# The inverse turn through DRAM to partitions 4 apart, a last stage on 64×32 tiles, and half of the loop's matrices made on the chip

## The chip, the cores and the metric

The kernel runs on one core of one Trainium2 chip. The metric is the device time of one execution in microseconds (us). All data are float32. TensorE (PE in the profile) multiplies matrices, its weight loads are listed apart (PEld). VectorE is DVE, ScalarE is ACT, GpSimd is POOL. SyncE (SP) does no arithmetic here, it issues transfers. POOL issues transfers too, on a queue of its own.

## The reference

Two branches read the same 2048×512 input and are mixed by a gate for each row:

```python
x = A_u
g = _sigmoid((x * gate_w).sum(-1, keepdims=True))
a = _A_ref(x, ...)   # K from 128 complex modes per channel; y = causal convolution of u with K; + u * Dskip
b = _B_ref(x, ...)   # gelu(x @ w1 + b1) @ w2 + b2, 512 -> 1792 -> 512
return g * a + (1 - g) * b
```

In `_A_ref`, `K = einsum(Cc, exp(dt*A*l), dt*Bc).real` gives 2048 taps for each of the 512 channels, and the convolution is done in the reference with a Fourier transform of length 4096.

## The kernel before

The kernel has two parts. `front` computes the taps, the dense branch, the gates, and the first stage of the forward transform of signal and taps. Its instructions are ordered by a planner (`Plan`), which the change leaves alone. `conv` does the rest, in an order written out by hand. Everything below is about `conv`.

The transform is split into 32 frequencies of the first stage (`n` in the code, taken in the order of `k0_order`) and 64 points of the second. `front` leaves the first stage's results in DRAM (`t2_d`), one block of 128 rows for each `n`. `conv` then works in three steps.

**The loop** (`for s in range(16)`) takes two `n` at a time. `fetch(n)` brings the block (`t2`, 512 KB) and, for every fourth `n`, the constant matrices of four `n` (`cc`, 512 KB) through SP. A block has 12 buffers. `signal(s)` and `taps(s)` (both through `pair`) multiply 128×64 matrices into two halves of a PSUM bank. ScalarE copies the taps' result to SBUF (`k`). `product(s)` is six VectorE instructions, the complex product of signal and taps. `inverse(s)` multiplies it back with 64-row matrices into `pa`. `turn(s)` copies each `pa` to `sa` on ScalarE (four buffers) and sends it off. In one iteration TensorE does `signal(s+1)`, `taps(s+2)`, `inverse(s)`. The product of `s` runs on VectorE meanwhile.

**The turn.** The last stage must sum over `n`, so all 32 `sa` tiles have to become one tile `t3` whose partitions run over `n`. Each `sa` has 128 rows, made of 4 parts `j` (real or imaginary, times two row halves `i`) of 32 rows `q`. In `t3`, one partition holds one `(n, j)` with all 32 `q` one behind another, 64 KB. `settle` does this in `GROUPS`: the first 28 `sa` are stored to `t4_d` in DRAM through SP, and when a group of 8, 8, 8 or 4 is complete, POOL reads it into `t3` at partitions 4, 4, 4 or 8 apart. The last four `sa` go straight from SBUF into 4 partitions each, 32 apart, also on POOL's queue, which works in order.

**The last stage** is 32 matrix products of 128 rows by 64 columns (half of each matrix is zero, since the two halves `i` don't mix), two for each of 16 output tiles. VectorE adds each, times the gate, to the dense result (`mo`), which `dense(k)` has read back from `out`, and SP stores it. Two of the dense branch's sums (42 products of 128×128 by 512) are left by `front` as a list `late`. `rest(n)` works off `n` entries (three products each): 4 in iteration 14, 4 in iteration 15, and the other 6 behind the loop.

PSUM tiles of the tag `pu` have four buffers, `pa` and `pk` two each.

Of the kernel before, what the change touches and what calls it, by code (L numbers as in the profile page):

```python
# [17 lines left out]
P = 128  # L18
L = 2048
# [68 lines left out]
def k0_order():  # L88
    return [8 * (n % 4) + n // 4 for n in range(32)]


# [12 lines left out]
def constants():  # L104


    def om(e4):
        a = 2.0 * np.pi * (np.asarray(e4) % (4 * L)) / (4 * L)
        return np.cos(a), -np.sin(a)

    k0 = np.arange(32)
    p = np.arange(32)
    q = np.asarray(slot_q())
    k1 = np.arange(64)
    qn = np.arange(64)
# [10 lines left out]
    g1 = np.zeros((2, 2, 32, 2, 32))  # L126
    for i in range(2):
        g1[i, 0, :, i] = er.T / L
        g1[i, 1, :, i] = ei.T / L
    g1 = g1.reshape(4, 32, 64)  # L130
    rows = np.zeros((P, 64))
    for first, count, at, step in GROUPS:
        for i in range(count):
            for j in range(4):
                rows[at + step * (4 * i + j)] = g1[j, k0_order()[first + i]]
    g1 = rows


    f2 = np.zeros((32, 2, 64, 2, 64))
    g2 = np.zeros((32, 2, 64, 64, 2))  # L140
    for k in range(32):
        er, ei = om(4 * (q[:, None] * k + 32 * np.outer(q, k1)) + q[:, None])
        f2[k, 0, :, 0], f2[k, 1, :, 0], f2[k, 0, :, 1], f2[k, 1, :, 1] = er, -ei, ei, er
        er, ei = om(4 * (qn[None] * k + 32 * np.outer(k1, qn)) + qn[None])
        g2[k, 0, :, :, 0], g2[k, 1, :, :, 0] = er, ei
        g2[k, 0, :, :, 1], g2[k, 1, :, :, 1] = -ei, er
    g2 = g2.reshape(32, P, 32, 2, 2).transpose(0, 1, 3, 4, 2)

    ko = k0_order()
    f2 = f2.reshape(32, P, P)[ko]  # L150
    g2 = g2[ko].reshape(16, 2, 2, 64, P).transpose(0, 2, 1, 3, 4).reshape(32, P, P)
    c2 = np.stack([f2, g2], 1).reshape(8, 4, 2, P, P).transpose(0, 3, 1, 2, 4)
# [111 lines left out]
def gated_mix(  # L264
# [22 lines left out]

    dt_d = dr.tile([1, D], F32, name="dt_d")
    t2_d = dr.tile([32, P, 2, D], F32, name="t2_d")
    t4_d = dr.tile([32, P, D], F32, name="t4_d")  # L290

# [738 lines left out]
    def conv(pool, ps, late):  # L1030

        t3 = pool.tile([P, 32, D], F32, name="t3", bufs=1)
        g1t = pool.tile([P, 64], F32, name="g1t", bufs=1)
        ko = k0_order()
        c4s, t2s = {}, {}

        def fetch(n):
            if n % 4 == 0:
                c4s[n // 4] = pool.tile([P, 4, 2, P], F32, tag="cc", name=f"cc{n}", bufs=3)
                nc.sync.dma_start(c4s[n // 4], c2[n // 4])  # L1040
            t2s[n] = pool.tile([P, 2, D], F32, tag="t2", name=f"t2{n}", bufs=N_T2)
            nc.sync.dma_start(t2s[n], t2_d[ko[n]])
            if n == 7:
                nc.sync.dma_start(g1t, g1)


# [3 lines left out]
        def pair(s, r, c, out):  # L1050

            for i in range(2):
                n = 2 * s + i
                w = c4s[n // 4][:, n % 4, 0, 64 * c : 64 * c + 64]
                nc.tensor.matmul(out[64 * i : 64 * i + 64], w, t2s[n][:, r], start=True, stop=True)  # L1055
# [17 lines left out]
        def product(s):  # L1073

            (ur, ui), (kr, ki) = pus.pop(s), fac.pop(s)
            z = [pool.tile([P, D], F32, tag=f"z{i}", name=f"z{s}{i}", bufs=1) for i in range(4)]
            v = [pool.tile([P, D], F32, tag=f"v{i}", name=f"v{s}{i}", bufs=2) for i in range(2)]
# [8 lines left out]
        def inverse(s):  # L1086
# [4 lines left out]
            for c in range(2):  # L1091
                n = 2 * s + c
                w = c4s[n // 4][:, n % 4, 1]
                for i in range(2):
                    r = slice(64 * i, 64 * i + 64)
                    nc.tensor.matmul(pas[2 * s + i], w[r], v[c][r], start=(c == 0), stop=(c == 1))  # L1096

        def settle(n, sa):

            for first, count, at, step in GROUPS:  # L1100
                if count > 1 and first <= n < first + count:
                    nc.sync.dma_start(t4_d[n], sa)
                    if n == first + count - 1:
                        rows = t4_d[first : n + 1].rearrange("n (j q) d -> (n j) q d", j=4)
                        nc.gpsimd.dma_start(t3[at:P:step], rows)
                elif n == first:
                    nc.gpsimd.dma_start(t3[at:P:step], sa)
# [28 lines left out]
        for n in range(N_T2):  # L1136
            fetch(n)
        nxt = N_T2
        taps(0)
        signal(0)  # L1140
        taps(1)
        for s in range(16):

            for n in range(nxt, min(2 * s + N_T2, 40)):
                (fetch if n < 32 else dense)(n if n < 32 else n - 32)
                nxt = n + 1
            product(s)
            if s + 1 < 16:
                signal(s + 1)
            if s + 2 < 16:  # L1150
                taps(s + 2)
# [9 lines left out]
        for t in range(16):  # L1161
            pb = ps.tile([P, D], F32, tag="pu", name=f"pb{t}", bufs=4)
            for b in range(2):
                nc.tensor.matmul(pb[64 * b : 64 * b + 64], g1t, t3[:, 2 * t + b], start=True, stop=True)  # L1164
            z, g = mos[t // 2][:, t % 2], gate[:, 0, t : t + 1]
            nc.vector.scalar_tensor_tensor(z, pb, g, z, ALU.mult, ALU.add)
            if t >= 12:
                nc.sync.dma_start(out[t], z)
            elif t % 2 == 1:
                nc.sync.dma_start(out[t - 1 : t + 1].rearrange("s p d -> p s d"), mos[t // 2])  # L1170

# [19 lines left out]
def layout(inputs):  # L1191
# [6 lines left out]

    xs = xpq.reshape(32, 16, 4, D).transpose(1, 2, 0, 3).reshape(16, P, D)
    xt = xs.reshape(NSB, SB, 4, P).transpose(0, 3, 2, 1)  # L1200
# [46 lines left out]
```

## Time and profile before

| what | us |
|---|---|
| median of 3 runs (lowest to highest) | 574.27 (571.66 to 575.11) |
| the profiled execution, its own time | 573.21 |
| its span, first to last instruction | 571.4 |
| `front`, up to the first product of `conv` | 434.8 |
| from there to the first `inverse` | 12.7 |
| from the first `inverse` to the end of the last | 86.7 |
| from there to the first product of the last stage | 15.9 |
| the last stage, to VectorE's last instruction | 17.7 |
| the last store and the end | 3.5 |

The stages' ends are read from the chain of waits and from the timeline of TensorE. The prediction shows the lines. In the table of stages a column is an engine's busy time in a stretch with the number of its instructions, then the clock that TensorE was granted (1.00 is full), the mean busy share of the 16 DMA engines, and GB/s. One matrix product of float32 shows as two MATMUL records. A source line such as L1164 is a line of the kernel before.

### The profile page before, as it was taken

The numbers are of one execution on the slowest core, as the hardware profiler recorded it, in microseconds if no ns is written. First come the engines' busy times: TensorE is split into PE (matmuls) and PEld (weight loads), VectorE is DVE, ScalarE is ACT, GpSimd is POOL, SyncE is SP. The second block draws the span as 40 slices with busy tenths as digits, with TensorE's granted clock in tenths as the row PEclk, the third lists the DMA queues.
The fourth block names the chain that finished last, engine by engine and source line by source line (L and its number), as shares of the span: only waits on it lengthen the run. The fifth ranks groups of instructions, "written<-read, shape, count | busy, mean of one in ns | idle before, by whom it ended". The sixth has DMA issues, their size and how long they took to land.

```text
span 571.4 us, 11957 instructions
## 1 busy us (share of the span) xinstructions
PE 541.3 (95%) x4746; PEld 403.8 (71%) x4746; DVE 449.4 (79%) x844; ACT 361.8 (63%) x606; POOL 32.2 (6%) x69
## 2 busy tenths in 40 slices
PE   7859999999999999999999999999998999999646
PEld 7738878888887888888888889898884333324412
DVE  5899998998989989998998898988512766675116
ACT  4998656899676799987669857477443334333100
POOL 2000000000000000000120201101010000000200
PEclk9969999999999999999999999999998999999959
DMA  8868735232864232649531358223269899999846
GB/s 267 306 216 304 240 111 186 75 130 86 255 209 167 95 130 93 201 141 252 137 82 33 95 122 156 75 38 80 35 143 334 320 322 396 380 420 452 230 97 258
DMA packets 77396, 109.50 MB, mean 192 GB/s; under 512 B 39014, under 2 KB 42218, under 8 KB 77228
## 3 DMA queue, kind: packets, MB, share of 16 engines
q1 hardware_dynamic: 71484, 87.89, 45.2%
q0 software_dynamic: 5856, 20.85, 14.6%
q8 instruction: 37, 0.61, 0.4%
q14 instruction: 19, 0.16, 0.1%
HBM read 63.09 MB, written 44.57 MB: 188 GB/s over the span
## 4 chain that ended last, share of the span: by engine, by line
PE 77%; DMA 14%; DVE 2%; ACT 2%; SPq 1%; issue 1%; POOL 0%; POOLq 0%; ACTq 0%
PE pk L647 11%; PE acc L905 9%; PE ph L857 9%; PE ph L859 8%; PE ph L858 8%; PE acc L907 8%; PE acc L906 8%; DMA t_d<-sa 5%; PE pu L388 4%; PE p2k L1055 3%; PE pb L1164 3%; DMA t<-t_d 3%; PE pa L1096 3%; PE p2u L1055 3%; DMA t<-sa 2%; DMA ld<-in_xt_dram 2%
## 5 line engine op out<-in xcount | busy, mean ns | idle before, releaser
L857 PE MATMUL ph<-xh,wh 128*128 128x256 f32 x448 | 128.0, 286 | 1.5 <-DVE wh L736 1.5
L859 PE MATMUL ph<-xh,wl 128*128 128x256 f32 x448 | 127.0, 283 | 0.6 <-DVE wl L740 0.5
L858 PE MATMUL ph<-xlo,wh 128*128 128x256 f32 x448 | 126.5, 282 | 0.0
L857 PEld LDWEIGHTS ph<-xh,wh 128*128 128x128 f32 x448 | 85.1, 190 | 7.5 <-issue 4.0
L905 PE MATMUL acc<-wh,hh 128*128 128x512 f32 x210 | 87.8, 418 | 0.4 <-ACT hh L877 0.4
L858 PEld LDWEIGHTS ph<-xlo,wh 128*128 128x128 f32 x448 | 85.1, 190 | 1.7
L859 PEld LDWEIGHTS ph<-xh,wl 128*128 128x128 f32 x448 | 85.1, 190 | 1.2 <-DVE wl L740 1.2
L906 PE MATMUL acc<-wl,hh 128*128 128x512 f32 x210 | 83.2, 396 | 0.0
L907 PE MATMUL acc<-wh,hl 128*128 128x512 f32 x210 | 82.9, 395 | 0.0
L874 ACT ACTIVATE ph<-ph,b1t 128x256 f32<-128x256 f32 x112 | 50.6, 452 | 28.7 <-PE ph L859 26.9
L647 PE MATMUL pk<-y,xc 128*32 128x64 f32 x2048 | 61.5, 290 | 0.0
L647 PEld LDWEIGHTS pk<-y,xc 128*32 128x32 f32 x2048 | 57.2, 136 | 4.0 <-issue 2.5
L905 PEld LDWEIGHTS acc<-wh,hh 128*128 128x128 f32 x210 | 39.8, 190 | 19.8 <-issue 11.9
L887 DVE TENSOR_TENSOR hl<-ph,hh 128x512 fp32r<-128x512 f32 (+1 forms) x62 | 38.2, 618 | 13.1 <-ACT hh L877 12.5
L907 PEld LDWEIGHTS acc<-wh,hl 128*128 128x128 f32 x210 | 39.8, 190 | 9.7 <-DVE hl L887 0.8
L611 DVE TENSOR_TENSOR y<-y,ea 128x64 f32<-128x64 f32 (+4 forms) x80 | 45.3, 566 | 0.4
L906 PEld LDWEIGHTS acc<-wl,hh 128*128 128x128 f32 x210 | 39.9, 190 | 5.8
L666 ACT COPY sk<-pu 128x512 f32<-128x512 f32 x32 | 33.9, 1129 | 15.5 <-PE pu L388 15.3
L1112 ACT COPY sa<-pa 128x512 f32<-128x512 f32 x32 | 17.7, 588 | 36.8 <-PE pa L1096 21.1
L877 ACT CAST hh<-ph 128x512 fp32r<-128x512 f32 (+1 forms) x62 | 33.0, 532 | 10.9 <-PE acc L906 9.1
L456 DVE TENSOR_TENSOR xt<-xc,zz 128x256 f32<-128x256 f32 (+2 forms) x48 | 37.2, 775 | 1.9 <-ACT xc L582 1.6
L1055 PE MATMUL p2k<-t,cc 128*64 128x512 f32 x128 | 35.4, 613 | 3.0 <-DMA t<-t_d 1.7
(138 smaller groups left out, 891.5 us busy)
## 6 DMA issues: line engine op xcount, KB each, us to landing
t<-t_d SPq DMA_DIRECT2D x32, 512.0 KB, 7.9
t_d<-st SPq DMA_DIRECT2D x32, 256.0 KB, 3.3
t_d<-sk SPq DMA_DIRECT2D x32, 256.0 KB, 4.2
t_d<-sa SPq DMA_DIRECT2D x28, 256.0 KB, 6.9
ld<-in_xt_dram SPq DMA_DIRECT2D x16, 256.0 KB, 3.9
xh_d<-xh SPq DMA_DIRECT2D x8, 512.0 KB, 3.8
xl_d<-xlo SPq DMA_DIRECT2D x8, 512.0 KB, 5.5
ux<-in_xl_dram SPq DMA_DIRECT2D x16, 256.0 KB, 3.4
```

The source lines that it names most:

```text
L456: vec(2 * m, lambda: vv.tensor_mul(t, a, br), due, [ka, *kb], [kt])
L611: nc.vector.tensor_mul(both(n, 64 - 3 * n, n), both(0, 64 - n, n), an)
L647: nc.tensor.matmul(pks[q][32 * j : 32 * j + 32, gg], x[:, r, :, ch], y[:, r, :, ch], start=(r == 0), stop=(r == 1), skip_group_check=True,)
L857: nc.tensor.matmul(p, h, xh[xk][:, d], start=(d == 0), stop=False)
L858: nc.tensor.matmul(p, h, xlo[xk][:, d], start=False, stop=False)
L859: nc.tensor.matmul(p, lo, xh[xk][:, d], start=False, stop=(d == 3))
L874: nc.scalar.activation(phs[q][:, n], phs[q][:, n], AF.Gelu_apprx_tanh, bias=b1t[:, f : f + 1])
L887: nc.vector.tensor_sub(lo, phs[q][:, 0:nf], hi.bitcast(F32))
L905: nc.tensor.matmul(a, h, wh[1][w], start=start, stop=False)
L906: nc.tensor.matmul(a, h, wl[1][w], start=False, stop=False)
L907: nc.tensor.matmul(a, l, wh[1][w], start=False, stop=(j == 3))
L1055: nc.tensor.matmul(out[64 * i : 64 * i + 64], w, t2s[n][:, r], start=True, stop=True)
```

## The change

Three things change, all in `conv` and in the constants and layouts that go with it. `front`'s instructions stand in the same order as before on every engine.

1. **The turn.** All 32 `sa` are stored to `t4_d`. The groups are 8, 8, 8, 4, 4. A new map `seat(n)` places `n`: `t3`'s partition is 64·`i` + `seat(n)` + 4·(real or imaginary), so within a group the partitions are 4 apart. A group of 8 is one read on POOL's queue whose target counts 32 partitions, while its source counts 2 halves `i` of 16 rows each. A group of 4 is two reads of 8 rows each, one for each `i`.
2. **The last stage.** Since `i` now divides the partitions in halves, a product has 64 rows and 32 columns, and the zeros are gone: 64 products, eight for a pair of output tiles, in row halves (`i`) and column quarters (`b`). Pairs of PSUM tiles come from `pu` and, every third time, from `pa`. Of the 16 results, VectorE adds 10. For the 6 in `ASIDE`, ScalarE multiplies by the gate into an old `z` tile, and POOL adds.
3. **The matrices.** The constants of four `n` are fetched as two transfers of 128 KB (`cf`, `cg`) in place of one of 512 KB. Three ScalarE instructions (`matrices(m)`) make the other half by copying or negating.

With these, `rest` is called with 3 entries in iteration 15 and none in 14, so 11 remain for behind the loop. The `dense` reads move from iterations 11 to 14 to behind the turns of iterations 13 to 15. The tiles `sa` and `z` are allocated first and `t3` after the first four blocks, so that the blocks take the room of other tiles of `front` than before.

```diff
-N_REST = 4
+N_REST = 3
-GROUPS = ((0, 8, 0, 4), (8, 8, 1, 4), (16, 8, 2, 4), (24, 4, 3, 8), (28, 1, 7, 32), (29, 1, 15, 32), (30, 1, 23, 32), (31, 1, 31, 32))
+GROUPS = ((0, 8), (8, 8), (16, 8), (24, 4), (28, 4))
+ASIDE = (1, 3, 6, 8, 11, 13)
+def seat(n):
+    return 8 * (n % 8) + n // 8
...
-                c4s[n // 4] = pool.tile([P, 4, 2, P], F32, tag="cc", name=f"cc{n}", bufs=3)
-                nc.sync.dma_start(c4s[n // 4], c2[n // 4])
+                f = pool.tile([P, 2, 4, 64], F32, tag="cf", name=f"cf{m}", bufs=4)
+                g = pool.tile([P, 2, 3, 64], F32, tag="cg", name=f"cg{m}", bufs=4)
+                nc.sync.dma_start(f[:, 0], c2[m, :, 0:256].rearrange("p (n k) -> p n k", n=4))
+                nc.sync.dma_start(g[:, :, 1:3], c2[m, :, 256:512].rearrange("p (s c k) -> p s c k", s=2, c=2))
...
+        def matrices(m):
+            f, g = c4s[m]
+            nc.scalar.mul(f[0:64, 1], f[64:128, 0], -1.0)
+            nc.scalar.copy(f[64:128, 1], f[0:64, 0])
+            nc.scalar.mul(g[:, :, 0], g[:, :, 2], -1.0)
...
         def turn(s):
             for n in (2 * s, 2 * s + 1):
-                sa = pool.tile([P, D], F32, tag="sa", name=f"sa{n}", bufs=4)
+                sa = sas[n % 4]
                 nc.scalar.copy(sa, pas.pop(n))
-                settle(n, sa)
+                nc.sync.dma_start(t4_d[n], sa)
+                for first, count in GROUPS:
+                    if n != first + count - 1:
+                        continue
+                    rows = t4_d[first : n + 1].rearrange("n (c i q) d -> i n c (q d)", c=2, i=2)
+                    if count == 8:
+                        nc.gpsimd.dma_start(t3[seat(first) : P : 4], rows)
+                    else:
+                        for i in range(2):
+                            at = 64 * i + seat(first)
+                            nc.gpsimd.dma_start(t3[at : at + 8 * count - 3 : 4], rows[i])
...
+            if n == 3:
+                t3 = pool.tile([P, 32, D], F32, name="t3", bufs=1)
+                g1t = pool.tile([P, 32], F32, name="g1t", bufs=1)
+        matrices(0)
...
-            else:
+            if s == 15:
                 rest(N_REST)
             inverse(s)
             turn(s)
+            for k in {13: (0,), 14: (1, 7), 15: (2, 3, 4, 5, 6)}.get(s, ()):
+                dense(k)
...
+        for m in range(8):
+            tag, n = ("pa", 2) if m % 3 == 2 else ("pu", 4)
+            pbs = [ps.tile([P, D], F32, tag=tag, name=f"pb{m}{i}", bufs=n) for i in range(2)]
+            for b in range(4):
+                for i in range(2):
+                    r = slice(64 * i, 64 * i + 64)
+                    nc.tensor.matmul(
+                        pbs[i][32 * b : 32 * b + 32], g1t[r], t3[r, 4 * m + b], start=True, stop=True
+                    )
+            for i in range(2):
+                t = 2 * m + i
+                z, g = mos[m][:, i], gate[:, 0, t : t + 1]
+                if t in ASIDE:
+                    a = zs[ASIDE.index(t) % 4]
+                    nc.scalar.mul(a, pbs[i], g)
+                    nc.gpsimd.tensor_add(z, z, a)
+                else:
+                    nc.vector.scalar_tensor_tensor(z, pbs[i], g, z, ALU.mult, ALU.add)
```

On TensorE, the end of the loop before: `p2u` is `signal(15)`, `acc` are products of `rest`, `pa` is `inverse`.

```order
L1055 MATMUL p2u_5546<-t_5349,cc_5303 64x512
L1055 MATMUL p2u_5546<-t_5351,cc_5303 64x512
L1131 MATMUL acc_5549<-wh_130,xh_119 128x512
L1132 MATMUL acc_5549<-wl_144,xh_119 128x512
L1133 MATMUL acc_5549<-wh_130,xlo_121 128x512
L1131 MATMUL acc_5549<-wh_131,xh_119 128x512
```

And now, at the same place behind `signal(15)`:

```order
L1067 MATMUL p2u_5493<-t_5331,cf_5289 64x512
L1067 MATMUL p2u_5493<-t_5333,cf_5289 64x512
L1107 MATMUL pa_5496<-v_5482,cg_5290 128x512
L1107 MATMUL pa_5497<-v_5482,cg_5290 128x512
L1107 MATMUL pa_5496<-v_5483,cg_5290 128x512
L1107 MATMUL pa_5497<-v_5483,cg_5290 128x512
L1142 MATMUL acc_5518<-wh_130,xh_119 128x512
```

The 12 products of `rest` that stood between `signal(15)` and `inverse(14)` are gone from there. Behind `inverse(14)` 9 stand now where 12 stood, and 33 behind the loop where 18 stood.

On POOL, the end of the program before (`t3` is the tile of the last stage, the size is the target's):

```order
L937 DMA out_0_dram<-io1_156 128x512
L1105 DMA t3_4842<-t4_d_62 32x16384 x3
L1105 DMA t3_4842<-t4_d_62 16x16384
L1107 DMA t3_4842<-sa28_5568 4x32x512
L1107 DMA t3_4842<-sa29_5571 4x32x512
L1107 DMA t3_4842<-sa30_5605 4x32x512
L1107 DMA t3_4842<-sa31_5608 4x32x512
```

And now:

```order
L1120 DMA t3_4862<-t4_d_61 32x1x16384 x3
L1124 DMA t3_4862<-t4_d_61 8x16384 x4
L1195 ISA
L1195 TENSOR_TENSOR mo0_5480<-mo0_5480,z0_4846 128x512
L1195 TENSOR_TENSOR mo1_5506<-mo1_5506,z1_4847 128x512
L1195 TENSOR_TENSOR mo3_5542<-mo3_5542,z2_4848 128x512
L1195 TENSOR_TENSOR mo4_5544<-mo4_5544,z3_4849 128x512
```

The four copies from `sa` became four reads of 8 rows from DRAM, and the reads of a group of 8 show the target cut as 32 by 1. Behind them stand an instruction (ISA) that reloads POOL's library of operations, and the additions.

On SP, the last rows ahead of the output before (`mo` are the `dense` reads):

```order
L1102 DMA t4_d_62<-sa22_5431 128x512
L1102 DMA t4_d_62<-sa23_5434 128x512
L1120 DMA mo2_5438<-out_0_dram 128x2x512
L1120 DMA mo3_5440<-out_0_dram 128x2x512
L1102 DMA t4_d_62<-sa24_5476 128x512
L1102 DMA t4_d_62<-sa25_5479 128x512
L1120 DMA mo4_5482<-out_0_dram 128x2x512
L1120 DMA mo5_5484<-out_0_dram 128x2x512
L1102 DMA t4_d_62<-sa26_5520 128x512
L1102 DMA t4_d_62<-sa27_5523 128x512
L1120 DMA mo6_5527<-out_0_dram 128x2x512
L1120 DMA mo7_5529<-out_0_dram 128x2x512
```

And now, from the stores of `sa` 26 and 27 on (the four `sa` tiles are taken in turn):

```order
L1114 DMA t4_d_61<-sa2_4844 128x512
L1114 DMA t4_d_61<-sa3_4845 128x512
L1131 DMA mo0_5480<-out_0_dram 128x2x512
L1114 DMA t4_d_61<-sa0_4842 128x512
L1114 DMA t4_d_61<-sa1_4843 128x512
L1131 DMA mo1_5506<-out_0_dram 128x2x512
L1131 DMA mo7_5508<-out_0_dram 128x2x512
L1114 DMA t4_d_61<-sa2_4844 128x512
L1114 DMA t4_d_61<-sa3_4845 128x512
L1131 DMA mo2_5540<-out_0_dram 128x2x512
L1131 DMA mo3_5542<-out_0_dram 128x2x512
```

Up to the store of `sa` 27 no `dense` read stands among the stores any more. Three stand ahead of the last two stores, five behind them.

More of the change, by code (lines that the diff above doesn't have):

```diff
@@ L123, in constants @@
     f1h, f1l = split12(np.concatenate([f1.reshape(64, P)] * 2, 0))
[L126 to L141, printed above, removed]
+    rows = np.zeros((2, 64, 32))
+    for n, k in enumerate(k0_order()):
+        rows[:, seat(n)] = er.T[k] / L
+        rows[:, seat(n) + 4] = ei.T[k] / L
+    g1 = rows.reshape(P, 32)
+    ko = k0_order()
+    f2 = np.zeros((32, 2, 64, 64))
+    g2 = np.zeros((32, 64, 2, 32, 2))
+    for n, k in enumerate(ko):
         er, ei = om(4 * (q[:, None] * k + 32 * np.outer(q, k1)) + q[:, None])
-        f2[k, 0, :, 0], f2[k, 1, :, 0], f2[k, 0, :, 1], f2[k, 1, :, 1] = er, -ei, ei, er
+        f2[n, 0], f2[n, 1] = er, -ei
         er, ei = om(4 * (qn[None] * k + 32 * np.outer(k1, qn)) + qn[None])
[L145 to L152, printed above, removed]
+        g2[n, :, 0], g2[n, :, 1] = (z.reshape(64, 32, 2) for z in (er, -ei))
+    f2 = f2.reshape(8, 4, P, 64).transpose(0, 2, 1, 3).reshape(8, P, 256)
+    g2 = g2.transpose(0, 1, 2, 4, 3).reshape(8, 2, P, P).transpose(0, 2, 1, 3).reshape(8, P, 256)
+    c2 = np.concatenate([f2, g2], 2)
     c1 = np.concatenate([f1h, f1l], 1)
@@ L1142, in conv @@
         for s in range(16):
-            for n in range(nxt, min(2 * s + N_T2, 40)):
-                (fetch if n < 32 else dense)(n if n < 32 else n - 32)
+            for n in range(nxt, min(2 * s + N_T2, 32)):
+                fetch(n)
                 nxt = n + 1
@@ L1159, in conv @@
             nc.vector.scalar_tensor_tensor(z, accs[s], gate[:, 1, 14 + s : 15 + s], z, ALU.mult, ALU.add)
[L1161 to L1170, printed above, removed]
+        for m in range(8):
[16 more added lines that the diff above has]
+                    nc.vector.scalar_tensor_tensor(z, pbs[i], g, z, ALU.mult, ALU.add)
+                if m >= 6:
+                    nc.sync.dma_start(out[t], z)
+            if m < 6:
+                nc.sync.dma_start(out[2 * m : 2 * m + 2].rearrange("s p d -> p s d"), mos[m])
     ctx.enter_context(tc.manual_schedule())
```

32 lines of the change are left out of this document (13 added, 19 removed).

## The prediction

> **What bounds the kernel now.** I read the chain of waits first, since it names what ended last. These are its lines from `conv` (start, duration, engine or DMA, line):
>
> ```profile
> 433.74 3.61 DMA t<-t_d
> 437.39 2.82 PE p2k L1055 x5
> ...
> 453.02 1.92 PE pa L1096 x8
> 454.93 1.87 PE p2u L1055 x8
> 456.80 1.72 PE p2k L1055 x8
> 458.52 1.92 PE pa L1096 x8
> ...
> 523.81 10.82 DMA t_d<-sa
> ...
> 537.84 12.13 DMA t<-sa
> 550.16 16.93 PE pb L1164 x64
> 567.11 0.75 DVE mo L1166
> ```
>
> There are three regimes: a start that waits for a block, a loop of 5.50 us per iteration (453.02 to 458.52) on TensorE, and a tail of two transfers and the last stage. The busy times of these stretches (PE, PEld, DVE, ACT, POOL, clock, DMA share, GB/s) say how tight each is:
>
> ```profile
> 434.80:437.40 2.60, 1.05 (x4) 0.20 (x4) 0.27 (x1) 0.00 (x0) 0.00 (x0) 0.86 0.92 334
> 437.40:440.01 2.61, 2.61 (x7) 0.76 (x9) 0.00 (x0) 0.58 (x1) 0.00 (x0) 0.50 1.01 397
> 447.50:520.65 73.15, 72.84 (x313) 23.24 (x313) 48.02 (x79) 29.21 (x52) 1.08 (x2) 1.00 0.97 368
> 520.65:534.23 13.58, 13.58 (x59) 6.98 (x57) 4.97 (x9) 2.74 (x5) 0.51 (x1) 1.00 1.03 416
> 534.23:550.16 15.93, 4.30 (x18) 3.25 (x19) 1.50 (x2) 1.08 (x2) 3.24 (x5) 0.76 0.79 149
> 550.16:567.86 17.70, 16.91 (x64) 5.64 (x64) 12.01 (x16) 0.00 (x0) 0.00 (x0) 0.83 0.53 203
> ```
>
> In the loop TensorE is busy 72.84 of 73.15 us, so no saving on transfers or ScalarE can shorten it. Between the last `inverse` (534.23) and the last stage TensorE works 4.30 of 15.93 us. The last stage itself is TensorE again, at a clock of 0.83.
>
> **The matrices and the loop.** Nothing of this is on TensorE. Three ScalarE instructions of at most this size come for every two iterations:
>
> ```profile
> L874 ACT ACTIVATE ph<-ph,b1t 128x256 f32<-128x256 f32 x112 | 50.6, 452 | 28.7 <-PE ph L859 26.9
> ```
>
> That is at most 1.4 us per 11 us, on an engine busy 29.21 of 73.15. I cost it at nothing, under the cover of TensorE's 5.50 us. Were that cover gone, because `cf` and `cg` land late, the copies `k` and `sa` queued behind them would wait too, and TensorE for those. SP issues eight transfers more, but moves 2.1 MB less. In the loop the DMA engines are at 0.97, so this is relief and no gain.
>
> **The start, −3.0.** SP's waits hold this line:
>
> ```profile
> SPq L1042 <- PE ph L859: 3.5, 1, 3.5
> ```
>
> Some blocks lie on tiles that `front`'s last products still read, and SP stood 3.5 us for that. In the new layout the blocks lie on the taps' tiles, read long before. So the second block can be asked for 3.5 us sooner. Without that wait TensorE would run two `taps`, two `signal` and one more `taps` from 434.84 on: 3 × 1.72 + 2 × 1.87 = 8.9 us, so `inverse(0)` at 443.7 in place of 447.51. That is 3.8 us, of which 1.1 are the stretch at clock 0.50 (2.61 us for 7 records of 0.215). Next in line is the transfer of blocks 2 and 3, with the DMA engines already at 0.92. I take 3.0, bounds 0 and 3.8.
>
> **The products of `rest`, −3.4.** The first and last of 12 in iteration 14, the last instruction of `product(15)` on VectorE among them, and what follows:
>
> ```profile
> 524.44 0.50 PE L1131 MATMUL acc<-wh,xh 128*128 128x512 f32 x1
> ...
> 526.75 0.69 DVE L1083 TENSOR_TENSOR v<-z,z 128x512 f32<-128x512 f32 x1
> ...
> 527.06 0.39 PE L1133 MATMUL acc<-wh,xlo 128*128 128x512 f32 x1
> 527.38 1.99 PE L1096 MATMUL pa<-v,cc 64*128 64x512 f32 x8
> ```
>
> A product takes 0.23 us (2.94 / 12, less a change of shape). Before the last `inverse` there were 24, now there are 9: 15 × 0.23 = 3.4. It is a gain only if VectorE keeps up. `inverse(15)` needs `product(15)`, done at 527.44. TensorE would come there at 524.44 + 1.99 + 9 × 0.23 = 528.5, so nothing waits. The last `inverse` then ends at 534.23 − 3.0 − 3.4 = 527.8. The 33 products behind it (7.6 us) run to 535.4 while the turn is under way.
>
> **The turn, −4.1.** Its rows: the landing times of the `sa` stores, of the group reads and of the direct copies, each with the line of its issues.
>
> ```profile
> L1102 SPq DMA_DIRECT2D t_d<-sa x28: 319/330/587, 450.1 to 523.8; - x28
> DMA to landing us min/median/max: 4.3/6.9/12.9
> ...
> L1105 POOL DMA_DIRECT2D t<-t_d x4: 490/522/541, 475.3 to 535.2; - x4
> DMA to landing us min/median/max: 9.3/9.3/11.2
> ...
> L1107 POOL DMA_DIRECT2D t<-sa x4: 664/686/732, 535.8 to 537.8; - x4
> DMA to landing us min/median/max: 12.1/12.8/13.6
> ```
>
> Before, `sa` 27 took 10.82 us behind the `dense` reads, POOL stood for it, and four copies of only 256 KB then took over 12 us. How fast a read can be is in two stretches, the second group's 2 MB read at 4 apart and the fourth group's 1 MB at 8 apart:
>
> ```profile
> 505.00:510.00 5.00, 5.00 (x26) 1.53 (x23) 3.69 (x6) 1.77 (x4) 0.00 (x0) 1.00 1.01 437
> 536.40:541.00 4.60, 2.13 (x10) 1.43 (x8) 1.50 (x2) 0.00 (x0) 2.10 (x4) 1.00 1.08 230
> ```
>
> At 437 GB/s the last megabyte takes 2.4 us. Now: two ScalarE copies 1.1; the store 5 (near the minimum of 4.3, since only three `dense` reads stand ahead of it and no block); issue of two reads 1.0; from issue to the first bytes 1.2 (535.22 to 536.4); 2.4 for the data; 1.1 to be seen (9.3 less 1.2 and 4.8 leaves 3.3 under load; here the queues are nearly empty). Sum 11.8, against 15.9. Bounds: 4.3 for the store gives 11.1, or −4.8; 12.9 for it and 11.2 for the read give 26.2, or +10.3. So the last stage starts at 527.8 + 11.8 = 539.6, and TensorE has idled since 535.4.
>
> **The last stage, −7.7.** Rows: VectorE's result, ScalarE's like `io`, and the narrowest products of the kernel.
>
> ```profile
> L1166 DVE SCALAR_TENSOR_TENSOR mo<-pb,gate,mo 128x512 f32<-128x512 f32 x16 | 12.0, 751 | 16.5 <-PE pb L1164 15.2
> L926 ACT ACTIVATE io<-acc,gate 128x512 f32<-128x512 f32 x30 | 20.5, 691 | 17.0 <-PE acc L907 16.6 <-DVE gate L800 0.4
> L812 POOL MEMSET ld<- 33x512 f32 x1 | 0.6, 552 | 0.0
> 63.30 3.77 PE pk L647 x127
> ```
>
> Before, two column halves run side by side: 8 records in 1.72 us (`p2k`), 0.215 a record. Now there are 128 records, and eight tiles could run together: 128 × 0.215 / 4 = 6.9 us. Issue isn't the bound (3.77 us for 127 records of L647, 128×32). VectorE has 10 × 0.75 = 7.5 us, and starts when the first pair is there (0.9): 8.4. ScalarE has 6 × 0.69 = 4.1. POOL's addition isn't in the trace: its one row of 512 columns is 0.55 with no input, VectorE's with two is 0.75. I take 1.2; at 1.5 its six (9 us) would set the end. After 4 us of idling the clock may be at half, as the rows show (0.50 behind a 1.5 us gap at the start, 0.83 here): +1.5. Total 10.0, bounds 8.4 and, if still only two tiles ran at a time, 128 × 0.215 + 0.75 = 28.3. The Trainium skill, page "TensorE: Matmul & The Clock Gate", section "Part 3: Packing small matmuls — row/col tiling", gives a measured speedup of 6.32 for nine tiles, short of nine; scaled to eight (an estimate, 5.6), the 64 products of 0.86 us would take 9.8 us and the sum would be 2 us longer. No run here shows eight tiles.
>
> **The sum.** Span 571.4 − 3.0 − 3.4 − 4.1 − 7.7 = 553.2, the end of 3.5 us unchanged. The profiled execution's own time was 573.21, 1.8 above its span, and the median 574.27 is 1.1 above that: 556.1, I say 556. This case's own range is 551 to 567: the low bounds together give 571.4 − 3.8 − 3.4 − 4.8 − 9.3 + 2.9 = 553, and the runs reach 2.6 below their median; the high end is no gain at the start (+3), four tiles at a time (128 × 0.215 / 2 + 0.75 = 14.5, +4.5) and 3 more in the turn.
>
> **The rivals.** First, **the group reads run on few DMA engines**, and the kernel gets slower. The queues during the second group's read (packets, MB, share of 16 engines):
>
> ```profile
> q0 software_dynamic: 32, 2.10, 96.7%
> q1 hardware_dynamic: 23, 0.09, 4.4%
> ```
>
> 32 packets of 64 KB (q0, POOL's) filled 16 engines for 4.84 us, and SP's queue (q1) got 23 packets through. So such a packet holds its engine for 2.4 us, and SP gets about one packet in between. The four direct copies were issued over 2.0 us and all landed within 0.5 us of 549.7 (535.8 + 13.6, 537.8 + 12.1). On all 16 engines, one behind the other, the first would have landed far ahead of the last. So each had engines of its own, about four. Their target counts 4 partitions, their source 128 rows. If the engines are the number into which both sides' outer counts divide, the new reads (32 and 2) get two engines; if the target alone decides, 16. On two, a read takes 8 × 4.84 = 38.7 us, in which SP's blocks, spread over all engines, stand behind it. The loop has a cushion of four `sa` tiles, two iterations, 11 us. The next group's stores wait in the same queues, so the three reads run in a row, each with some 8 us for stores and start: 472 + 3 × 47 = 613, two more reads with their stores 20, last stage 10, end 3.5, and 2.9 outside the span: 649. It decides from where a read exceeds the cushion, at four engines (19 us). For it: the copies above. Against it: they fit the target's count as well. I give it 0.30. The Trainium skill, page "DMA: Bandwidth & Descriptors", section "Why a DMA increments its semaphore by 16 and not by 1", states the first reading (the largest number up to 16 that divides the slowest dimension of both sides), and an exception by which direct copies from GpSimd spread by partitions over 16. By that rule the copies had four engines, and the trace agrees; which branch the new reads take, no row shows.
>
> Second, **the turn isn't shortened**: the store behind the `dense` reads takes its 12.9, the read its 11.2, 26.2 − 11.8 = 14 us more: 570. The first group's 9.3 for 2 MB and the emptier queue speak against it. 0.05.
>
> Third, **the tiles don't overlap beyond two**: 28.3 in place of 10.0, 574. The 64-row products (1.92 for 8 records) show that rows and columns each give two, none shows both. 0.05.
>
> **How the numbers follow.** Forecast 0.60, rivals 0.30, 0.05, 0.05. Within 1% (568.5 to 580) is about what a measurement of this kernel can tell from no change; there lie the second and third. Faster 0.61, same 0.09, slower 0.30. As the first rival holds too much to be left out, the range goes from 551 to the middle of it, 650; half of it, 0.15, is left out above.
>
> **What would show it.** Right: no wait of PE on `t<-t_d` at the start; `inverse(15)` some 6 us sooner; group reads landing in about 9 us; `pb` from about 540, for under 11 us. Wrong: group reads landing after 40 us with waits of ScalarE on `t_d<-sa` in the loop (first rival); a store of `sa` 31 over 10 us (second); `pb` records at 0.2 us each (third); or POOL's additions last in the chain.

## The result and the profile after

The changed kernel takes **675.75 us** (median of 4 runs, 675.28 to 677.11), the kernel before 574.69. The ratio is 1.1775, its 95% interval 1.173 to 1.182: slower by 18%, past the end of the range, where a gain of 18 us was forecast. It went the way of the first rival, and by 27 us more than the rival's price.

The chain of waits of the changed kernel (start, duration, engine or DMA, line):

```profile
444.89 1.92 PE pa L1107 x8
...
469.99 45.74 DMA t_d<-sa
...
516.47 3.78 PE pa L1107 x6
...
531.06 47.61 DMA t<-t_d
...
588.83 41.97 DMA t_d<-sa
...
637.61 8.42 DMA mo<-out_dram
...
646.86 9.00 DMA t<-t_d
...
655.91 5.82 PE pb L1186 x49
```

Up to 469 us the loop runs at 5.50 us per iteration, ahead of before: `inverse(0)` begins at 444.9. Then three waits of 42 to 48 us stand in it. Each falls on one of the reads of eight matrices, as the answer on their line shows (issues, first and last; issue to landing):

```profile
L1120 POOL DMA_DIRECT2D t<-t_d x3: 576/617/638, 469.0 to 586.7; - x3
...
DMA to landing us min/median/max: 43.9/46.6/47.7
```

How many engines such a read has is in a stretch in which almost nothing else moves, 484 to 506. In the view of windows (PE, PEld, DVE, ACT, POOL, clock, DMA share, GB/s):

```profile
484.00:506.00 22.00, 2.07 (x2) 0.50 (x2) 0.61 (x2) 0.58 (x1) 0.00 (x0) 0.58 0.13 55
```

and in the view of the queues, POOL's (packets, MB, share of 16 engines):

```profile
q0 software_dynamic: 18, 1.18, 12.4%
```

12.4% of 16 engines is 1.98: two engines, at 54 GB/s together (1.18 MB in 22 us; the 55 in the row holds SP's transfers as well). 18 packets of 64 KB on two engines in 22 us make 2.44 us a packet, as in the kernel before. The transfers on SP's queue stand behind them: that queue moves 0.03 MB in these 22 us, and ScalarE waits for the stores of `sa` (us in all, times, longest):

```profile
ACT sa L1113 <- DMA t_d<-sa: 112.0, 6, 37.2
```

| us from the span's start | before | after |
|---|---|---|
| `inverse(0)` begins | 447.44 | 444.82 |
| last `inverse` ends | 534.23 | 635.32 |
| first `pb` begins | 550.16 | 653.3 |
| last result of the last stage | 567.86 | 667.13 |
| span | 571.4 | 674.3 |

The start gained 2.6 us, the loop lost 103.7, and the tail from the last `inverse` to the end takes 39.0 us where it took 37.2.

### The profile page after: what moved, and what is told of

The parts are those of the page before. It is cut to its first block, busy times and chain, and to the rows that moved or that the text cites. A ratio compares the mean times of both kernels' runs of the same rounds, so it can differ in the third digit from the quotient of the medians.

```text
span 674.3 us, 12160 instructions
## 1 busy us (share of the span) xinstructions
PE 549.4 (81%) x4810; PEld 405.1 (60%) x4810; DVE 445.2 (66%) x838; ACT 375.2 (56%) x636; POOL 38.8 (6%) x74
## 4 chain that ended last, share of the span: by engine, by line
PE 63%; DMA 26%; ACT 5%; DVE 2%; SPq 2%; issue 1%; POOL 0%; POOLq 0%; ACTq 0%
DMA t_d<-sa 13%; DMA t<-t_d 9%; PE pk L646 9%; PE acc L904 7%; PE ph L856 7%; PE ph L858 6%; PE ph L857 6%; PE acc L906 6%; PE acc L905 6%; PE pu L387 4%; PE pa L1107 3%; PE p2k L1067 3%; PE p2u L1067 3%; DMA mo<-out_dram 1%; SPq L680 1%
## 5 line engine op out<-in xcount | busy, mean ns | idle before, releaser
L1107 PE MATMUL pa<-v,cg 64*128 64x512 f32 x128 | 40.5, 694 | 61.2 <-ACT sa L1113 61.2
L1090 DVE TENSOR_TENSOR z<-p2u,k 128x512 f32<-128x512 f32 x16 | 11.1, 691 | 103.4 <-PE p2u L1067 96.2
L1107 PEld LDWEIGHTS pa<-v,cg 64*128 64x128 f32 x128 | 13.4, 209 | 87.1 <-ACT sa L1113 66.5
L1067 PE MATMUL p2k<-t,cf 128*64 128x512 f32 x128 | 37.0, 637 | 34.2 <-DMA t<-t_d 32.4
L886 DVE TENSOR_TENSOR hl<-ph,hh 128x512 fp32r<-128x512 f32 (+1 forms) x62 | 38.1, 616 | 13.8 <-ACT hh L876 13.2
L1067 PEld LDWEIGHTS p2k<-t,cf 128*64 128x64 f32 x128 | 10.4, 145 | 56.5 <-issue 46.6
```

Source lines behind the costliest of these rows:

```text
L886: nc.vector.tensor_sub(lo, phs[q][:, 0:nf], hi.bitcast(F32))
```

## The experiments

**The reads alone, on the kernel before.** Theory: a read gets as many engines as divide the outer counts of both its sides. The first two kernels change nothing in the kernel before but the order of the 32 rows in its three reads of eight matrices, and the order of the rows of `g1` with it:

```diff
-rows = t4_d[first : n + 1].rearrange("n (j q) d -> (n j) q d", j=4)
+rows = t4_d[first : n + 1].rearrange("n (i c q) d -> c (n i) (q d)", i=2, c=2)   # e3: 2 and 16
+rows = t4_d[first : n + 1].rearrange("n (j q) d -> j n (q d)", j=4)              # e4: 4 and 8
...
 nc.gpsimd.dma_start(t3[at:P:step], rows)
```

> The kernel before, with nothing of the change but the order of the 32 rows in its three reads of eight matrices (and of the rows of the constant g1 that go with them): the source now counts 2 and 16, the target 32 as ever; same bytes, same packets, same partitions. Theory: 2 engines, 44 to 48 us a read, ScalarE and SP stand for them, the loop ends some 100 us later: about 670 us (640 to 690). Rival (it is the rest of the change that makes the reads slow): no change, 571 to 577 us.

Measured: 680.91 us, ratio 1.1847 (1.179 to 1.1905). Its reads on their line (three of them slow; the 22.3 is the fourth, of another form):

```profile
DMA to landing us min/median/max: 22.3/49.7/54.3
```

and POOL's queue between 490 and 520 us:

```profile
q0 software_dynamic: 24, 1.57, 12.1%
```

Again 12.1% of 16, two engines. An order of rows, with the same bytes and the same partitions, costs 107 us on a kernel that has nothing else of the change. That the rest of the change made the reads slow is out.

> As the run with 2 and 16 on the kernel before, but the source counts 4 and 8. Theory: 4 engines of 8 packets each, 8 x 2.42 = 19.4 us at the least and about 24 with the 7 us by which the two-engine reads exceeded 38.7 scaled down; with 8 us for stores and start a group takes some 32 us where the loop gives it 22, less a cushion of 11 once: about 590 us (577 to 615). Rival (any source that does not count as its target does falls to one or two engines): as slow as 2 and 16, over 640. Rival (the target alone decides): no change.

Measured: 666.43 us, ratio 1.1625 (1.1577 to 1.1673), far from the 590 expected. POOL's queue between 499 and 511 us:

```profile
q0 software_dynamic: 13, 0.79, 23.7%
```

and the landing times of the reads on their line (the 9.0 is again the fourth read, of another form):

```profile
DMA to landing us min/median/max: 9.0/43.0/47.5
```

23.7% of 16 is 3.8: it does have four engines, so the target alone does not decide. With the target at 32 in all these runs, the source alone could be the rule. Against that stand only the direct copies of the kernel before, whose sources count 128: by their landing times they had about four engines each. No run tells "divides both" from "the smaller of the two". But 0.79 MB are 12 packets of 64 KB, and 3.8 engines for 12 us make 3.8 us a packet instead of 2.42. The read is hardly shorter. The engines are there, and each is slower. The trace does not say to which partitions a packet goes; by the order of the rows the four engines write, at any time, partitions 32 apart.

The Trainium skill, page "DMA: Bandwidth & Descriptors", section "Why a DMA increments its semaphore by 16 and not by 1", takes the largest number up to 16 that divides the slowest dimension of both sides: 2 and 4 here, as measured. The Trainium skill, page "SBUF — State Buffer", section "Door 1: The DMA port swizzle (why `[64,N]` ≈ `[32,N]`)", says that partitions 32 apart share a port and that partitions 0 to 63 reach only 8 of 16 ports. The slower packets (3.8 us for 2.42) agree with it, and so does the next run.

**The changed kernel with the reads split by halves.**

```diff
-if count == 8:
-    nc.gpsimd.dma_start(t3[seat(first) : P : 4], rows)
-else:
-    for i in range(2):
+for i in range(2):
     at = 64 * i + seat(first)
     nc.gpsimd.dma_start(t3[at : at + 8 * count - 3 : 4], rows[i])
```

> The changed kernel, but each of the three reads of eight matrices is written as two, one for each half of the partitions, so that its source counts 16 rows and its target 16 partitions. Theory (a read gets as many engines as divide the outer counts of both its sides, 2 before this edit): 16 engines each, landing after about 10 us instead of 44 to 48, no wait of ScalarE on the stores of sa in the loop, the last inverse near 528, pb from about 540, the whole about 556 us (551 to 567), the first forecast. Rival (the loop is held by something else that the change brought: eight more transfers on SP, the matrices on ScalarE, the seats 4 apart): the waits of 40 us stay, above 640 us.

Measured: 584.64 us, ratio 1.0175 (1.0133 to 1.0217). The 40 us waits are gone, 91 of the 101 us with them, but the forecast of 556 does not come. Its chain still has three waits in the loop:

```profile
477.26 13.41 DMA t_d<-sa
...
502.08 15.89 DMA t_d<-sa
...
524.36 12.93 DMA t_d<-sa
```

and POOL's queue during the first read, from 472 to 484 us, shows why:

```profile
q0 software_dynamic: 48, 2.10, 82.2%
```

82.2% of 12 us is 9.9 us of all 16 engines for 2.10 MB. The kernel before needed 4.84 us for as much (32 packets, 96.7% of 5.00 us). A read of 16 rows to one half of the partitions has its 16 engines, and runs at half rate. So did the fourth group of the kernel before, 16 rows to partitions 8 apart over all 128 (230 GB/s, all engines busy). One half of the partitions is therefore not the whole rule, and no run tells the partitions that are written from the mere count of 16 rows. Is that enough to explain 10 us? The same split, on the kernel before, alone:

```diff
-nc.gpsimd.dma_start(t3[at:P:step], rows)
+for h in range(0, count, 4):
+    rows = t4_d[first + h : first + h + 4].rearrange("n (j q) d -> (n j) q d", j=4)
+    a = at + 16 * h
+    nc.gpsimd.dma_start(t3[a : a + 15 * step + 1 : step], rows)
```

> The kernel before, with nothing changed but that each of its three reads of eight matrices is issued as two, 16 rows to the lower and 16 to the upper half of the partitions. Theory (half rate is what holds the loop in e1_split): packets of about 4.9 us in place of 2.4, 10 to 11 us a group in place of 6.6, ScalarE waits on stores, and 8 to 12 us more than the kernel before: 583 us (578 to 590). Rival (it is something else of the change): 572 to 576 us.

Measured: 585.18 us, ratio 1.0201 (1.0169 to 1.0233). ScalarE's waits (line, released by, us in all, times, longest):

```profile
ACT sa L1114 <- DMA t_d<-sa: 44.5, 11, 7.7
```

and in the kernel before:

```profile
ACT sa L1112 <- DMA t_d<-sa: 15.5, 5, 5.2
```

Half-rate reads by themselves cost this kernel 11 us; its loop has its DMA engines at 0.97. e1_split has the same reads and the whole rest of the change besides, and loses as much: so the rest of the change gave it nothing that the time shows, which is the second question.

**Reads of eight rows.** Two ways to avoid 16 rows in one half: groups of four throughout, or groups of eight read in four pieces.

```diff
-GROUPS = ((0, 8), (8, 8), (16, 8), (24, 4), (28, 4))
+GROUPS = ((0, 4), (4, 4), (8, 4), (12, 4), (16, 4), (20, 4), (24, 4), (28, 4))    # e5
+for h in range(0, count, 4): ...  # e6: groups as they were, rows of matrices first + h to first + h + 3
```

> The changed kernel with eight groups of four matrices in place of 8, 8, 8, 4, 4, so that each read is two of 8 rows, to 8 partitions 4 apart. Theory (what is left of the loss in the loop after e1_split comes from reads of 16 rows to 16 partitions of one half, whose packets took 4.87 us where the reads of 8 rows took 2.42): packets of 2.4 to 2.9 us, no wait of ScalarE on the stores of sa, the last inverse 528 to 531; the turn still some 20 us, because the store of sa 31 stands behind the dense reads (12.6 us in e1_split); in all about 570 us (563 to 577). Rival (any packet of 64 KB holds SP's blocks and stores up, whatever its target): the three waits of 13 to 16 us in the loop stay, 581 us or more.

> The groups of 8, 8, 8, 4, 4 as in the changed kernel, but each read of eight matrices is issued as four reads of 8 rows, one after the other. Theory (the spread over partitions counts, not the number of matrices per group): the loop as in e5_fours, packets of 2.4 to 2.9 us, 570 us (563 to 577), within 1% of e5_fours. Rival (it is the size of the group, 2 MB at once, that stalls the loop): as e1_split, 581 us or more.

Measured: 586.41 us (1.0207, 1.0178 to 1.0235) and 586.21 us (1.0218, 1.0186 to 1.0249). No time was won, and the theory as I had put it fell. The last two reads of e5 stand alone in the trace, in a window:

```profile
559.60:564.50 4.90, 1.65 (x2) 0.18 (x2) 0.00 (x0) 0.00 (x0) 0.00 (x0) 0.50 0.48 208
```

and in POOL's queue over the same time:

```profile
q0 software_dynamic: 24, 0.98, 46.5%
```

0.98 MB are 15 packets, and 46.5% of 16 engines for 4.90 us make 2.43 us a packet: full rate, but on 7.4 engines. The reads are issued 0.5 us apart. In the trace eight packets start within 0.25 us, and the other eight start as these end, from 562.02 on: the two reads of a pair take turns on eight engines. Eight engines at full rate and sixteen at half rate come to the same 208 to 213 GB/s, whichever way a group was cut here.

**The dense reads, the results of ScalarE and POOL.** Both on top of e5_fours:

```diff
-for k in {13: (0,), 14: (1, 7), 15: (2, 3, 4, 5, 6)}.get(s, ()):
+for k in {10: (0,), 11: (1, 2), 12: (3, 4), 13: (7,), 15: (5, 6)}.get(s, ()):     # e7
-ASIDE = (1, 3, 6, 8, 11, 13)
+ASIDE = ()                                                                          # e8
```

> e5_fours with the dense reads earlier: one in iteration 10, two in 11, two in 12, one in 13, two behind the last store, where the changed kernel has one in 13, two in 14 and five behind the last store. Theory (the turn is long because the last stores stand behind dense reads): the store of sa 31 lands in about 5 us instead of 12.6, pb starts 7 us sooner than in e5_fours, about 561 us (555 to 568). Rival (the loop has no room for them, or the turn is held by the group read itself): no gain over e5_fours, or a loss.

> e5_fours with no rows put aside for ScalarE and POOL: all 16 results of the last stage are VectorE's. Theory (VectorE's 0.75 us a result would set the end, POOL's six additions of 1.27 us run beside it): the last stage takes 0.9 + 16 x 0.75 = 12.9 us instead of about 10, so 3 us more than e5_fours. Rival (TensorE at half clock sets the pace, or POOL's additions are what ends last): within 1 us of e5_fours, or faster.

Measured: 585.04 us (1.0192, 1.0165 to 1.0219) and 585.44 us (1.0207, 1.018 to 1.0234), both rivals. In e7 ScalarE's waits on stores grew from 20.0 to 28.9 us: the loop had no room for them. That sixteen results on VectorE cost no more than ten, with six on POOL, is taken up below.

**One full-rate read per group.** For a source of 32 rows one behind the other, `sa` must be turned out with the halves outermost, and stored half by half:

```diff
-t4_d = dr.tile([32, P, D], F32, name="t4_d")
+t4_d = dr.tile([4, 2, 8, 64, D], F32, name="t4_d")
-nc.sync.dma_start(t4_d[n], sa)
+for i in range(2):
+    nc.sync.dma_start(t4_d[n // 8, i, n % 8], sa[64 * i : 64 * i + 64])
...
+rows = t4_d[first // 8].rearrange("i n (c q) d -> (i n c) q d", c=2)
+nc.gpsimd.dma_start(t3[seat(first) : P : 4], rows)
```

> The changed kernel with four groups of eight, each read by one transfer whose source and target both count 32 rows, as in the kernel before, to the changed kernel's seats. For that sa is turned out in the order half, part, row (the constants' order, and one more ScalarE instruction per four matrices), and stored by two transfers of 128 KB, to an order in DRAM in which the 32 rows of a group lie behind one another. Theory (16 rows to one half, or 8 rows twice on the same 8 engines, run at half rate, 10 to 13 us per 2 MB where the loop has no such room; 32 rows over all partitions take 4.8 to 6.6): ScalarE waits on stores of sa for less than 5 us in all, the last inverse near 530, pb near 548, the whole about 566 us (560 to 573). Rival (the extra transfers of the constants, or the stores and reads through the same queue whatever their rate, hold the loop): the waits of 13 us stay, 580 us or more.

> e9_one with the dense reads earlier, as in e7_dense. Theory (in the tail the last stores stand behind dense reads; with the loop free again there is room for them in it): the turn 5 to 7 us shorter than in e9_one, about 560 us (554 to 568). Rival (the loop has no room): ScalarE waits on the stores of sa in iterations 11 to 14, no gain over e9_one.

Measured: 575.82 us (1.0025, 0.9999 to 1.0052) and 572.72 us (0.9996, 0.9968 to 1.0023). POOL's queue during the second read of e9, 502 to 507 us:

```profile
q0 software_dynamic: 32, 2.03, 94.4%
```

ScalarE's waits:

```profile
ACT sa L1117 <- DMA t_d<-sa: 13.8, 5, 5.7
```

and the stores' line (issue min/median/max in ns, first and last):

```profile
L1119 SPq DMA_DIRECT2D t_d<-sa x64: 445/588/3180, 447.6 to 538.5; - x64
```

2.03 MB again take 4.7 us of 16 engines, and the waits fall below before's 15.5. So the half rate was the rest of the loss against the kernel before (e10 shows its price alone). But the whole is only level with it, 10 to 13 us above what I expected of these two. e9 keeps 2.5 us at the start; its loop, from `inverse(0)` to the end of the last, takes 88.1 us where the kernel before took 86.8 with 15 products more in it.

The price of this form is 64 stores of 0.59 us in SP's queue in place of 32 of 0.32. Whether that holds the loop, I tried on e11 (e9 with the `dense` reads earlier) by issuing them from ScalarE:

```diff
-    nc.sync.dma_start(t4_d[n // 8, i, n % 8], sa[64 * i : 64 * i + 64])
+    nc.scalar.dma_start(t4_d[n // 8, i, n % 8], sa[64 * i : 64 * i + 64])
```

> e11_one_dense with the stores of sa issued from ScalarE's queue in place of SP's. Theory (the 64 stores of 0.59 us each stand in SP's one queue behind the blocks' and the dense reads' waits, which holds sa, and with it the loop's end and the last read): the waits of SP and ScalarE on each other go, the last inverse ends near 529 instead of 535, pb starts 4 to 6 us sooner, about 567 us (562 to 572). Rival (the data and not the issue is what the stores wait for, or the issues delay ScalarE's copies as much): 571 us or more.

Measured: 597.96 us (1.0414, 1.0382 to 1.0447). Worse: the issues keep ScalarE from its other work, and TensorE waits for the matrices that ScalarE makes:

```profile
PE p2k L1071 <- ACT cf L1058: 19.0, 6, 5.5
```

This shows that ScalarE has no room for the issues, not whether SP's queue is the limit; that stays open.

**The end of the last stage.** On e11 (e13), and on e12 (e14):

```diff
-ASIDE = (1, 3, 6, 8, 11, 13)
+ASIDE = (1, 3, 6, 8)
```

> e11_one_dense with 4 rows for ScalarE and POOL in place of 6 (the rows 11 and 13 go back to VectorE). Theory (POOL's last addition ends the stage, and three stores of SP stand behind it): VectorE's last result ends about 1 us after the last product, POOL is done before that, 2 to 4 us less than e11_one_dense: about 569.5 us. Rival (VectorE's 12 results of 0.75 us become the end): within 1 us of e11_one_dense.

> e12_actq and e13_aside4 together. Theory: both gains, about 564 us (559 to 570), faster than the kernel before by 1 to 2%. Rival (ScalarE with the issues becomes late for the copies k): 570 us or more.

Measured: e13 573.40 us (0.9985, 0.996 to 1.001), e14 598.11 us (1.0422, 1.04 to 1.0444). e13 is within 1 us of e11, though its last result no longer comes from POOL. In the profiled executions the stage with its end is 1.8 us shorter (17.9 against 19.7); the medians do not show it. Its last stage in four windows:

```profile
549.20:553.40 4.20, 4.19 (x56) 1.43 (x64) 1.50 (x2) 1.37 (x2) 1.28 (x1) 0.66 0.00 0
553.40:557.00 3.60, 3.60 (x72) 1.54 (x64) 3.50 (x6) 1.38 (x2) 3.16 (x3) 1.00 0.76 284
557.00:560.20 3.20, 0.76 (x16) 0.00 (x0) 3.17 (x5) 0.00 (x0) 0.64 (x1) 1.00 1.01 380
560.20:563.40 3.20, 0.00 (x0) 0.00 (x0) 0.00 (x0) 0.00 (x0) 0.00 (x0) 0.83 1.02 378
```

and the group of its products (count, busy time, mean ns of one):

```profile
L1186 PE MATMUL pb<-t,g1t 64*32 64x512 f32 x128 | 8.6, 687 | 7.5 <-DMA t<-t_d 7.5
```

and, for comparison, the second half of the kernel before's last stage and what follows it:

```profile
560.00:567.86 7.86, 7.07 (x34) 2.34 (x30) 6.89 (x10) 0.00 (x0) 0.00 (x0) 1.00 0.85 322
567.86:571.40 3.54, 0.00 (x0) 0.00 (x0) 0.00 (x1) 0.00 (x0) 0.00 (x0) 0.78 0.45 175
```

The tiles do what was hoped: 64 products in 8.6 us, where the kernel before took 16.9. But the results must also leave: 16 stores' worth, 4.19 MB, at 380 GB/s, take 11.0 us, and the DMA engines are full from 557 to 563.4, while the engines of the core have their last result at 560.2. The first store is issued 4.2 us after the first product, the bytes take 11.0, and 2.7 are left, ahead of the first byte and behind the last: 17.9 us from `pb` to the end, against 21.2 before. With a DMA share of 0.85 the kernel before was already near that bound. That would also be why moving results between VectorE and POOL did not change the time (e8, e13); no run varies the outputs alone.

**The products of `rest`, alone, on the kernel before.**

```diff
-else:
-    rest(N_REST)
+if s == 15:
+    rest(3)
```

> The kernel before with the change's treatment of the products of rest alone: 9 ahead of the last inverse in place of 24 (none in iteration 14, 3 times 3 in iteration 15). Prediction's term: the last inverse ends 15 x 0.23 = 3.4 us sooner and the products run in the turn, where TensorE idles: 571 us, 3.4 less than before. Rival (in the tail the stores of sa and the dense reads on SP's queue set the turn, not the last inverse): the last inverse ends sooner and pb starts when it did, no gain, 573 to 576.

Measured: 573.75 us (1.0011, 0.9986 to 1.0036): nothing. Three rows of its time line (TensorE's last `inverse`, the copies of `sa`, the last stage; idle time before, and what ended it, in brackets):

```profile
527.61 1.99 PE L1096 MATMUL pa<-v,cc 64*128 64x512 f32 x8
...
533.07 1.23 ACT L1112 COPY sa<-pa 128x512 f32<-128x512 f32 x2 [6.53 <-DMA t_d<-sa]
...
549.41 16.76 PE L1164 MATMUL pb<-t,g1t 128*64 128x512 f32 x64 [12.08 <-DMA t<-sa]
```

The last `inverse` begins 4.6 us sooner than the 532.24 of before, as the term said and more; the copies of `sa` begin 1.2 us sooner (533.07 against 534.30), since their buffers still wait for stores; `pb` begins 0.75 us sooner. The chain of e15 goes from the store of `sa` 27 (522.77, 10.83 us) through POOL's queue to the direct copies, past the last `inverse`.

Do the dense reads ahead of those stores hold them? e15 with four of the eight (7, 4, 5, 6) issued behind the last turn:

> e15_before_rest with four of the eight dense reads issued behind the last turn instead of in iterations 13 and 14. Theory (in the kernel before, too, the turn is set by the stores of sa, which stand behind the dense reads, and not by the last inverse): ScalarE no longer waits 6 us for the buffers of sa, the fourth group's read is issued at about 528 instead of 534, the direct copies at 530 to 533, pb at 543 to 545, 568 to 570 us. Rival (the direct copies take their 12 us beside the dense reads wherever these stand): pb at 548 or later, 572 to 576.

Measured: 578.14 us (1.008, 1.0057 to 1.0104), worse by 0.8%. The store of `sa` 27 is 1.8 us faster, but the direct copies are now beside the dense reads:

```profile
525.16 9.01 DMA t_d<-sa
...
537.35 16.93 DMA t<-sa
```

16.93 us where they took 12.13. The rival holds, and at a higher price: in both places of the tail that were tried, something of the turn stands behind the dense reads.

## Why the prediction was wrong

**The step that failed first** is the choice between the two readings of the direct copies. The forecast went by the reading in which the target alone decides, 16 engines and about 9 us a read, and left 0.30 for the other. The runs show that the source counts: with a target of 32, sources that count 2, 4 and 32 had 2, 4 and 16 engines, and the reads of the changed kernel took 46.6 us on two. The mechanism of the rival was right, to the 2.4 us a packet. Its price was low, mostly because a read took 46.6 us instead of 38.7 and the three were issued 59 us apart (469.0 to 586.7 for two steps) instead of 47: the rival's sum has `pb` at 633, and it began at 653.3. The last stage and the end, 13.8 and 7.2 us for 10 and 3.5, make up the rest.

**"At 437 GB/s the last megabyte takes 2.4 us"** failed too. The 437 were 32 rows over all partitions. The row beside it, 230 GB/s for 16 rows, was in the same fence and went into no term. Two reads of eight rows went at 208. With 16 engines for every read of eight matrices, the half rate still left the kernel about 2% slower (e1, e10).

**The start, −3.0**: the mechanism was right, the size somewhat less. SP's wait for `front`'s last products is in none of the 11 traces with the new layout. `inverse(0)` begins 2.6 us sooner in the changed kernel; over all traces it begins at 444.8 to 447.1 with the new layout and at 446.7 to 449.0 with the old, 2.0 us apart in the mean.

**The matrices, nothing**: on the path only behind a stall. In e9 TensorE waits 2.8 us in all for `cf`, after ScalarE has stood for a store; in the free loop nothing is lost. e12 shows what it costs without that cover.

**`rest`, −3.4**: on the kernel before the size was right and the path wrong (e15). The step "it is a gain only if VectorE keeps up" left out the stores. The chain of before, quoted at the head of the prediction, passes from `t_d<-sa` to `t<-sa` without the last `inverse` in it. In the changed kernel and in e9 the last `inverse` is on the chain, but the loop ends late there; in e13 the chain passes beside it, since the last two copies of `sa` wait for a store until 534.6 and the `inverse` ends at 534.0.

**The turn, 11.8**: 18.0 us in the changed kernel, 20.7 in e9, 15.2 in e13. Two terms failed. The store at 5 us "since only three dense reads stand ahead of it" took 9.8 in the changed kernel, and in e1 the last two took 12.6 and 12.8. The two reads behind it, forecast at 5.7 us from the first issue to the last landing, took 9.5. In e9 the last store took only 4.2 us, but it was issued 4.8 us after the copy of `sa` 31 had ended, behind other work on SP's queue, and the read of 2 MB took 10.3. So the second rival (the turn is not shortened) came true as well, in the changed kernel by the two terms that it names.

**The last stage, −7.7**: the products went as forecast, 6.9 us at full clock and 1.5 for the clock against 8.6 in e13 and 9.9 in e9, whose first 5 us ran at 0.50. POOL's addition was 1.28 instead of 1.2. At full clock eight records start together, within 0.1 us, and the next eight 0.43 us later (e13, from 552.3 on): 0.054 us a record, which is the 0.215 of two tiles divided by four. The estimate scaled from a figure of the Trainium skill, page "TensorE: Matmul & The Clock Gate", section "Part 3: Packing small matmuls — row/col tiling", was 9.8 us, or 0.077 us a record; the trace does not agree with that scaling, all eight tiles ran side by side. What is late next was not asked: the outputs. "The end of 3.5 us unchanged" became 6.9 in e13, and stage and end together gain 3.3 us.

Of the 18 us forecast, the best form that I ran (e13; its profiled execution was the fastest of its runs) shows 4.3 in its span: 2.3 at the start, 0.8 in the turn, 3.3 in the last stage with its end, less 2.1 in the loop, where 3.4 had been looked for. By its median it is level with the kernel before. Why its loop loses 5.5 us to the forecast is not settled: ScalarE waits there 16.7 us for stores (15.5 before), and no run tells SP's issues from the bytes.

## What to carry to other kernels

Before a transfer is reshaped, write down the outer count of its source and of its target as the instruction has them, and the partitions that are written at one time: in these runs the first set how many DMA engines worked, and how fast each was went with the second. When a stage bound by an engine is made faster, work out its bytes at the rate the trace shows; here 4.19 MB at 380 GB/s take 11.0 us, more than the products. And a gain on the step that ends last by the program's order counts only if the chain of waits goes through it.

## What the runs showed that was not expected

- Four engines that, by the order of the rows, write partitions 32 apart were hardly faster than two: 66 GB/s (0.79 MB in 12 us) against 54, and 41.5 to 47.5 us a read against 43.9 to 47.7.
- Sixteen rows to one half of the partitions go at half rate: 9.9 us of 16 engines for 2.10 MB against 4.84, and in a loop with DMA engines at 0.97 that is 2% of the whole kernel (e10).
- Two reads of eight rows issued behind one another shared eight engines (7.4 of 16 by their share), while the four direct copies of the kernel before, by their landings within 0.6 us, each had engines of their own.
- Eight 64×32 tiles ran fully side by side: 64 products of 512 columns in 8.6 us, and at full clock eight records each 0.43 us.
- A store of 64 partitions took SP 0.59 us to issue, one of 128 partitions 0.32.
